# Attention output with queries on partitions and denominators as a V column, turned through DRAM

## The chip, the cores and the metric

The kernel runs on one core of a Trainium2 chip. A core has a matrix engine (PE, TensorE) that multiplies a stationary operand, loaded into the array by a weight load, with a moving operand, and writes to PSUM; a vector engine (DVE), an activation engine (ACT) and GpSimd (POOL) that work element by element; and SP, which here only issues DMAs. Each engine has its own instruction stream and works through it strictly in the order in which it was written; the streams meet at semaphores. A DMA is issued by an engine's queue and carried out by 16 DMA engines that all queues share.

The metric is the device time of one execution, in microseconds (us). Times of one instruction are in nanoseconds (ns) where that is marked.

## The reference, cut to what matters

The reference is one transformer block on a sequence of 2048 tokens with 448 features: a modulated layernorm, a sliding dilated attention with 16 heads of 28 features, a residual, a second modulated layernorm and an MLP (448 to 1792 to 448) with another layernorm in front, and a second residual. The part that the change touches is this:

```python
qkv = (h @ wqkv).reshape(B, S, 3, H, Dh)            # q, k, v: 16 heads of 28
idx = pos[:, None] - (arange(8) * 2)[None, :]       # 8 keys, two apart, back from the query
logits = einsum('bhsd,bhswd->bhsw', q, k[idx]) * Dh ** -0.5   # masked where idx < 0
attn = softmax(logits, axis=-1)
o = einsum('bhsw,bhswd->bhsd', attn, v[idx])
x = x + ga * (o.reshape(B, S, 448) @ wo)
```

Since keys are two apart, even and odd tokens never meet: the kernel treats them as two sequences of 1024 tokens with a dense window of 8 keys. `ga` is a row of 448 numbers, computed from the conditioning vector `c`; the kernel multiplies it into `wo` once.

## The kernel before, in words

**Layout.** The 2048 tokens are 16 blocks of 128 (8 of even, 8 of odd tokens). `front_ln` normalizes a block, turns it on PE (`ptr`) and writes the features-on-partitions array `hT`; `front_qk` makes `qT` and `kT` from it (`pq`, L640). Attention runs in 9 steps, `attention(b)`, b = 0 to 8. A step holds two superblocks (n = 0, 1) of 114 queries, and a superblock two windows (j = 0, 1) of 57 queries that see 64 keys each.

**One attention step.** `values` (L692) makes V for the 128 keys of a superblock's two windows: DVE first copies the two overlapping windows of `hT` side by side into `hw` (L702), then four matmuls with `hw` as the 128-column stationary operand and `Wv` as moving operand (448 columns) accumulate V into `pv` (L708), and ACT copies it to `vbuf`, head by head, each head padded from 28 to 32 columns with zeros (L712). `lmm` (L733) computes the logits, keys on partitions: 64 small matmuls `lt`, each on a 32x64 part of the array. ACT takes the exponential (`et`, L743, two halves) and DVE multiplies with the band mask (L751, two halves). `dmm` then does two things, on 64x32 parts of the array: a matmul with a matrix of ones sums `et` over keys (`pd`, L765, 8 matmuls of 464 columns, 12 in the steps with a sequence's first window) and 64 matmuls with V as stationary operand give the unnormalized output `po` (L773), head features on partitions and queries along the free axis. ACT turns the sums into reciprocals with a logarithm and an exponential (L785, L788); DVE multiplies (L798, two halves) and writes `oT`, which already has features on partitions.

**After attention.** `out_proj(t)` for each of the 16 token blocks takes 128 columns of `oT` as stationary operand and `wo_s` as moving operand, four matmuls `pw` (L814). `wo_s` keeps each head's 28 rows in a group of 32, so it is loaded by four DMAs into a tile zeroed by POOL, and scaled by `ga` on DVE (L676). The result goes through the residual (L818), two layernorms on DVE and POOL, and a DMA transpose from `ybuf` to `yT` (L840). `mlp(j)` works on two token blocks at a time: 56 matmuls with `w1` (`p`, L864), GELU on ACT, 28 matmuls with `w2` (`p`, L885), the last residual (L892) and the store (L905).

**Order.** Nothing runs in the order of the source. Every piece of work is an `add(engine, cost, function, ...)`; a planner (`Planner`) makes a list schedule from the costs written in these calls, from buffer counts (`ROOM`) and from an assumed extra delay of each DMA (`late`), tries it with 60 perturbed rankings, and emits each engine's stream in the order of the best. It adds a cost `SWITCH` when PE changes the way its array is divided (`mode`). So each stream is fixed before the run, and changing one cost can reorder all of them. `PHASES` says which attention steps are followed by which MLP pairs; ACT loads another function table between the two kinds. Dummy matmuls (`pwm`, L506) fill PE's early waits. `mods` computes the modulation rows (`pb`), sends them through a DRAM tile `mod_hbm` to get them onto all partitions (`mod_bc`, L671), and issues the loads of the MLP weights after that (`load_mlp`). All DMAs but one are issued by SP.

**DMA semaphores.** The DMAs of SP take eight semaphores in turn. A DMA that is to use a semaphore waits until the DMA eight places ahead of it has landed.

Of the kernel before, what the change touches and what calls it, by code (L numbers as in the profile page):

```python
# [11 lines left out]
FP32 = mybir.dt.float32  # L12
# [18 lines left out]
OTW = NSB * SBQ  # L31
NBLK = S // 128
EPS = 1e-5
DEN_SCALE = 2.0 ** -32
# [12 lines left out]
LMM, DMM = 0.55, 0.80  # L47
FILL_UNTIL, FILL_SHARE = 12.0, 1.0
ROOM = {"L": 2, "S": 4, "et": 2, "den": 2, "zh": 6, "yT": 3, "hm": 3, "vb": 4, "hw": 3}
# [229 lines left out]
def kernel(  # L279
# [41 lines left out]
    oT = cst.tile([128, 4, OTW], BF16, name="oT")  # L321
    Wv = cst.tile([128, KT, D], BF16, name="Wv")
    Wqk = cst.tile([128, KT, 2, H, HP], BF16, name="Wqk")
    wo_s = cst.tile([128, 4, D], BF16, name="wo_s")
# [12 lines left out]
    ones_k = cst.tile([128, 2, HP], BF16, name="ones_k")  # L337
    neg_half = cst.tile([128, 4], FP32, name="neg_half")
    den_bias = cst.tile([128, 1], FP32, name="den_bias")
# [19 lines left out]
    vbufs = [cst.tile([128, H, HP], BF16, name=f"vbuf{i}") for i in range(NV)]  # L359
# [65 lines left out]
    zero(1.6, lambda: wo_s[:], ["wo"], eng="POOL", rank=440)  # L425
    wo_v = A_wo.rearrange("(ft r d) n -> r d ft n", r=4, d=DH)
    for r in range(4):
        load(lambda r=r: nc.sync.dma_start(out=wo_s[HP * r:HP * r + DH, :, :], in_=wo_v[r]), D * D // 2, [f"wo{r}"],
             reads=["wo"])
# [38 lines left out]
    pool(0.1, lambda: nc.gpsimd.memset(den_bias[:], math.log(DEN_SCALE)), ["den_bias"])  # L468
# [18 lines left out]
    def consts():  # L487
        for vb in vbufs:
            nc.gpsimd.memset(vb[:, :, DH:HP], 0.0)
        nc.gpsimd.memset(ones_k[:], 1.0)  # L490
        nc.gpsimd.memset(ones_k[0:WIN - 1, 1, :], 0.0)

    pool(0.9, consts, ["ones", "vpad"])
# [10 lines left out]
    def dummy(n):  # L504
        for k in range(n):
            nc.tensor.matmul(pwm.t[:, k % 2, :], lhsT=warm_w[:, 0:128], rhs=warm_w[:], start=True, stop=True)  # L506
# [148 lines left out]
    def mods():  # L655
# [19 lines left out]
        for i in range(2):  # L675
            add("DVE", 0.55, lambda i=i: nc.vector.tensor_tensor(  # L676
                out=wo_s[:, 2 * i:2 * i + 2, :], in0=wo_s[:, 2 * i:2 * i + 2, :],
                in1=ga_bc.unsqueeze(1).to_broadcast([128, 2, D]), op=ALU.mult),
                reads=["ga"] + [f"wo{r}" for r in range(4)], writes=[f"wos{i}"], port=True)
# [12 lines left out]
    def values(sb_i):  # L692
# [3 lines left out]
        vbuf = Buf("vb", lambda k: vbufs[k], "vb")  # L696
        pv = ps_one([128, D], "pv")
        hw = sb("hw", [128, KT, 2, WK], BF16, "hw")

        def windows():  # L700
            h = hT[:, :, k0:k0 + WK]
            nc.vector.tensor_copy(out=hw.t[:], in_=bass.AP(h.tensor, h.offset, [h.ap[0], h.ap[1], [WQ, 2], [1, WK]]))  # L702

        P.wrote(add("DVE", 0.21, windows, port=True, reads=PADK + [f"h{kt}_{t}" for kt in range(KT) for t in tb], bufs=[hw]), hw)

        def vmm():
            for kt in range(KT):
                nc.tensor.matmul(pv.t[:], lhsT=hw.t[0:KE[kt], kt].rearrange("p j k -> p (j k)"), rhs=Wv[0:KE[kt], kt, :],  # L708
                                 start=(kt == 0), stop=(kt == KT - 1))

        P.wrote(add("PE", 0.757, vmm, reads=["wva", "wvb", "Wv0"], bufs=[pv, vbuf, hw]), pv)
# [5 lines left out]
    def attention(b, tbl, prev_w1):  # L717
# [4 lines left out]
        et = sb("et", [128, 4, 2, 4, WE], BF16, "et")  # L722
# [19 lines left out]
        for half in range(2):  # L742
            ex = add("ACT", 0.825, lambda half=half: nc.scalar.activation(  # L743
                out=et.t[:, 2 * half:2 * half + 2].rearrange("p r n ft c -> p r (n ft c)"),
# [4 lines left out]
            def msk(half=half):  # L749
                ev = et.t[:, 2 * half:2 * half + 2].rearrange("p r n ft c -> p (r n ft) c")  # L750
                nc.vector.tensor_tensor(out=ev, in0=ev, in1=mask[:], op=ALU.mult)  # L751

            add("DVE", 0.56, msk, port=True, bufs=[et], reads=["mask"], writes=[(et, half)])
        pd = ps_big("pd")
        pos = [ps_one([128, 2, 4, WQ], "po") for _ in range(2)]
        first = [s % (NSB // 2) == 0 for s in sbs]

        def dmm():
            for j in range(2):
                rows = slice(WK * j, WK * j + WK)  # L760
                edge = j == 0 and any(first)
                for n0, n1 in ((0, 1), (1, 2)) if edge else ((0, 2),):
                    ones = ones_k[rows, 1 if edge and first[n0] else 0, :]
                    for r in range(4):
                        nc.tensor.matmul(pd.t[HP * r:HP * r + HP, j, n0 * SBE:n1 * SBE], lhsT=ones,  # L765
                                         rhs=et.t[rows, r, n0:n1].rearrange("p n ft c -> p (n ft c)"),
                                         start=True, stop=True, tile_position=(WK * j, HP * r))
            for n in range(2):
                for ft in range(4):
                    for j in range(2):  # L770
                        rows = slice(WK * j, WK * j + WK)
                        for r in range(4):
                            nc.tensor.matmul(pos[j].t[HP * r:HP * r + HP, n, ft, :],  # L773
                                             lhsT=vb[n].t[rows, ft * 4 + r, :], rhs=et.t[rows, r, n, ft, 0:WQ],
                                             start=True, stop=True, tile_position=(WK * j, HP * r))

        P.wrote(add("PE", DMM, dmm, dense=0.3, reads=[(et, 0), (et, 1), "ones"], bufs=[et, *vb, pd, *pos], mode="64x32"), pd, *pos)
        lt_mms.append(P.tasks[-1])
        lden = sb("den", [128, 2, 2, 4, WE], FP32, "lden")
        rden = lden  # L780

        def flat(t):
            return t[:].rearrange("p j n ft c -> p j (n ft c)")

        P.wrote(add("ACT", 0.825, lambda: nc.scalar.activation(out=flat(lden.t), in_=pd.t[:, :, 0:2 * SBE], func=ACT.Ln,  # L785
                                                               scale=DEN_SCALE),
                    bufs=[pd, lden], order_after=[tbl]), lden)
        ex = add("ACT", 0.92, lambda: nc.scalar.activation(out=rden.t[:], in_=lden.t[:], func=ACT.Exp, scale=-1.0,  # L788
                                                           bias=den_bias[:]),
                 bufs=[lden], reads=["den_bias"], order_after=[tbl])  # L790
        P.wrote(ex, rden)
        exps.append(ex)
        o0 = b * 2 * SBQ

        def div(j):
            out = oT[:, :, o0 + j * WQ:o0 + j * WQ + WQ]
            out = bass.AP(out.tensor, out.offset, [out.ap[0], [SBQ, 2], out.ap[1], [1, WQ]])
            nc.vector.tensor_tensor(out=out, in0=pos[j].t[:],  # L798
                                    in1=rden.t[:, j, :, :, 0:WQ], op=ALU.mult)

        for j in range(2):
            add("DVE", 0.55, lambda j=j: div(j), bufs=[pos[j], rden],
                writes=[f"o{o0 + n * SBQ + j * WQ + i}" for n in range(2) for i in range(WQ)])


    y_of = {}

    def out_proj(t):
        c0 = t // 8 * (OTW // 2) + t % 8 * 128
        pw = ps_one([128, D], "pw")  # L810

        def mm():
# [168 lines left out]
```

## Time and profile before

| | |
|---|---|
| time, median of 2 runs | 186.7 us (186.02 and 187.38) |
| profiled execution, span from first to last instruction | 184.8 us |
| the profiled execution's time outside its span | not recorded; the two timed runs are 1.2 and 2.6 us above the span |
| PE busy with matmuls | 173.5 us, 94% |
| DVE, ACT, POOL busy | 124.6, 103.8, 47.5 us |
| first matmul with `w1` | 54.0 us |
| last matmul ends | 180.6 us |
| granted TensorE clock | full from 7.8 us on |

The profile is of one execution. Busy time is the time in which an engine has at least one instruction under way; a matmul's recorded duration holds its run through the array, so matmuls that follow each other overlap, and the rate is read from start to start or from the pieces of the chain of waits. The chain is followed back from the last instruction: at each step to what released it, or to the instruction ahead of it on its engine. An idle time whose releaser is "issue" is one in which the engine waited for nothing that the profile shows. A DMA's time to landing is counted from its issue to its last completion mark.

### The profile page before, as it was taken

Reading aid. Unit: us, or ns where it says so; the run is one execution under the profiler, and the core shown is the slowest. Engines: PE = TensorE matmul, PEld = TensorE weight load, DVE = VectorE, ACT = ScalarE, POOL = GpSimd, SP = SyncE. Lnnn points to the kernel's source line nnn. Section 1 sums busy time; section 2 is a strip of 40 time slices with the busy share of each in tenths; the row PEclk is TensorE's granted clock in tenths of the full one; section 3 lists DMA queues with packets and bytes.
Section 4 is the critical chain, followed back from the end, with each engine's and each line's share of the span. In section 5 each row is a group of like instructions: output and inputs, shape, how many; then the busy total and the mean of one; then the engine's idle time right before and its main releaser. Section 6 shows DMA issues by size and latency. Waiting matters only on the chain.

```text
span 184.8 us, 5433 instructions
## 1 busy us (share of the span) xinstructions
PE 173.5 (94%) x2325; PEld 111.5 (60%) x2333; DVE 124.6 (67%) x348; ACT 103.8 (56%) x139; POOL 47.5 (26%) x97
## 2 busy tenths in 40 slices
PE   3997789899999999999999999999999999999991
PEld 0574565455458655775855567678556756857750
DVE  3799599889899799688424389693346968711102
ACT  2167667767486877766585667426786530521230
POOL 7074000508501602334200060532001526200000
PEclk9999999999999999999999999999999999999999
DMA  5999779900110101301210100213001012040101
GB/s 172 304 356 265 193 175 313 326 14 7 27 32 0 28 5 32 82 0 28 42 18 0 52 5 4 57 50 48 14 4 53 0 32 78 0 103 7 51 0 50
DMA packets 19004, 13.99 MB, mean 76 GB/s; under 512 B 9246, under 2 KB 18403, under 8 KB 18980
## 3 DMA queue, kind: packets, MB, share of 16 engines
q1 hardware_dynamic: 18978, 13.64, 27.7%
q8 instruction: 18, 0.29, 0.7%
q14 instruction: 6, 0.05, 0.1%
q10 hardware_dynamic: 2, 0.00, 0.0%
HBM read 9.70 MB, written 1.84 MB: 62 GB/s over the span
## 4 chain that ended last, share of the span: by engine, by line
PE 90%; DVE 4%; issue 2%; DMA 1%; ACT 1%; DVEq 0%
PE p L864 27%; PE p L885 23%; PE pq L640 13%; PE pv L708 7%; PE pw L814 7%; PE pwm L506 3%; PE lt L733 3%; PE po L773 3%; PE ptr L607 1%; PE pd L765 1%; DMA yT<-ybuf 1%; DVE st_all L513 1%; DVE kT L649 1%; ACT lden L788 1%; PE pb L661 0%
## 5 line engine op out<-in xcount | busy, mean ns | idle before, releaser
L864 PE MATMUL p<-yT,w_s 128*128 128x256 bf16 x448 | 52.3, 272 | 0.1
L871 ACT ACTIVATE hm<-p 128x1024 bf16<-128x1024 f32 (+1 forms) x32 | 28.8, 916 | 36.8 <-PE p L864 36.8
L864 PEld LDWEIGHTS <-w_s 128*128 128x128 bf16 x448 | 43.3, 97 | 8.9 <-issue 0.6
L885 PE MATMUL p<-w_s,hm 128*128 128x448 bf16 x224 | 46.9, 353 | 0.0
L531 POOL TENSOR_TENSOR rs_all<-tv_all,neg_half 128x1 f32<-128x1 f32 (+1 forms) x35 | 20.9, 605 | 52.3 <-DVE tv_all L528 47.5
L885 PEld LDWEIGHTS <-hm 128*128 128x128 bf16 x224 | 21.2, 98 | 17.9
L844 POOL TENSOR_TENSOR x1p_ring<-x_all,gbb_bc 128x448 f32<-128x448 bf16 x16 | 17.2, 1079 | 54.6 <-DVE x_all L818 45.3
L640 PE MATMUL pq<-hT,Wqk 128*128 128x512 bf16 (+3 forms) x153 | 30.0, 334 | 0.5 <-issue 0.2
L892 DVE TENSOR_TENSOR x_all<-p,x1p_ring 128x448 bf16<-128x448 f32 x16 | 9.8, 618 | 26.0 <-PE p L885 26.0
L640 PEld LDWEIGHTS <-Wqk 128*128 128x128 bf16 (+1 forms) x160 | 15.1, 97 | 11.5 <-DVE Wqk L626 0.2
L513 DVE BATCH_NORM_STATS2 st_all<-x_all 128x6 f32<-128x448 bf16 x32 | 19.1, 617 | 0.7 <-DMA x_all<-in_A_x_dram 0.5
L743 ACT ACTIVATE et<-lt 128x928 bf16<-128x928 f32 x18 | 16.0, 941 | 5.0 <-PE lt L733 4.9
L708 PE MATMUL pv<-Wv,hw 128*128 128x448 bf16 x72 | 16.4, 353 | 1.6 <-DVE hw L702 0.9
L751 DVE TENSOR_TENSOR et<-et,mask 128x928 bf16<-128x928 bf16 x18 | 11.7, 649 | 5.3 <-ACT et L743 5.3
L814 PE MATMUL pw<-wo_s,oT 128*128 128x448 bf16 x64 | 14.4, 352 | 0.0
L712 ACT CAST vbuf<-pv 128x448 bf16<-128x448 f32 x18 | 9.6, 532 | 6.3 <-PE pv L708 6.2
L818 DVE TENSOR_TENSOR x_all<-pw,x_all 128x448 bf16<-128x448 f32 x16 | 9.9, 620 | 4.4 <-PE pw L814 4.2
L785 ACT ACTIVATE lden<-pd 128x928 f32<-128x928 f32 x9 | 8.5, 948 | 7.1 <-PE pd L765 7.1
L652 ACT CAST kT<-pq 128x512 bf16<-128x512 f32 (+1 forms) x14 | 7.1, 510 | 8.6 <-PE pq L640 8.2
L708 PEld LDWEIGHTS <-hw 128*128 128x128 bf16 x72 | 6.7, 97 | 7.7 <-issue 1.2
L798 DVE TENSOR_TENSOR oT<-po,lden 128x456 bf16<-128x456 f32 x18 | 10.6, 623 | 0.6 <-ACT lden L788 0.6
L833 DVE BATCH_NORM_STATS2 st_all<-h 128x6 f32<-128x448 bf16 x16 | 9.8, 621 | 0.1
(83 smaller groups left out, 172.3 us busy)
## 6 DMA issues: line engine op xcount, KB each, us to landing
out_dram<-x_all SPq DMA_DIRECT2D x8, 224.0 KB, 2.0
w_s<-in_B_w_dram SPq DMA_DIRECT2D x2, 784.0 KB, 12.3
wmod<-in_w_mod_dram SPq DMA_DIRECT2D x2, 672.0 KB, 7.5
w_s<-in_B_w_dram SPq DMA_DIRECT2D x1, 1344.0 KB, 9.1
x_all<-in_A_x_dram SPq DMA_DIRECT2D x1, 896.0 KB, 7.9
wm_st<-in_w_mod_dram SPq DMA_DIRECT2D x1, 720.0 KB
wqk_st<-in_A_wqkv_dram SPq DMA_DIRECT2D x2, 339.0 KB, 5.7
x_all<-in_A_x_dram SPq DMA_DIRECT2D x2, 224.0 KB
```

What stands on the lines that cost most here:

```text
L513: add("DVE", 0.53, lambda: nc.vector.bn_stats(out=st_all[:, sl, :], in_=src()), reads=key, writes=[f"st{sl}"])
L531: lambda: nc.gpsimd.tensor_tensor(out=rs_all[:, which, b0:b0 + n], in0=tv_all[:, which, b0:b0 + n], in1=neg_half[:, 0:n], op=ALU.pow),
L640: nc.tensor.matmul(pq.t[:], lhsT=wqk_m(kt, m), rhs=hT[0:KE[kt], kt, c0:c0 + n], start=(kt == 0), stop=(kt == KT - 1))
L708: nc.tensor.matmul(pv.t[:], lhsT=hw.t[0:KE[kt], kt].rearrange("p j k -> p (j k)"), rhs=Wv[0:KE[kt], kt, :], start=(kt == 0), stop=(kt == K ...
L743: ex = add("ACT", 0.825, lambda half=half: nc.scalar.activation(out=et.t[:, 2 * half:2 * half + 2].rearrange("p r n ft c -> p r (n ft c)") ...
L751: nc.vector.tensor_tensor(out=ev, in0=ev, in1=mask[:], op=ALU.mult)
L798: nc.vector.tensor_tensor(out=out, in0=pos[j].t[:], in1=rden.t[:, j, :, :, 0:WQ], op=ALU.mult)
L814: nc.tensor.matmul(pw.t[:], lhsT=oT[:, ft, c0:c0 + 128], rhs=wo_s[:, ft, :], start=(ft == 0), stop=(ft == 3))
L844: nc.gpsimd.tensor_tensor(out=x1p_ring[:, t % NX1P, :], in0=x_all[:, t, :], in1=gbb2_bc[:], op=ALU.add)
L864: nc.tensor.matmul(p1.t[:, f // 2, f % 2 * 256:f % 2 * 256 + 256], lhsT=w1_s[0:kp, kt, (fq + f) * 128:(fq + f + 1) * 128], rhs=yT.t[0:kp, ...
L871: gl = add("ACT", 0.18 + nf * 0.183, lambda fq=fq, nf=nf, p1=p1: nc.scalar.activation(out=hm.t[:, fq:fq + nf, :], in_=p1.t[:, 0:nf // 2, : ...
L885: nc.tensor.matmul(p2.t[:], lhsT=hm.t[:, ft, bi * 128:(bi + 1) * 128], rhs=w2_s[:, ft, :], start=(ft == 0), stop=(ft == FT - 1))
```

## The change

It is four edits that belong together.

1. `values` no longer copies windows. Eight matmuls take the two windows straight from `hT` as stationary operands of 64 columns each, one on the left and one on the right half of the array (parts of 128x64). `hw` and its DVE copy go.
2. `vbuf` gets ones in the columns behind each head's 28 features. `pmm` takes the place of `dmm`: 64 matmuls on 64x64 parts of the array, with `et` as stationary operand (64 keys by 64 queries) and 29 columns of V as moving operand, so that queries come out on partitions, 28 features and the denominator side by side. `pd`, `ones_k`, the logarithm and the exponential on ACT go; DVE takes a reciprocal of 32 columns and one product of 896 columns.
3. The output now has queries on partitions and has to be turned. Four DMAs of 57 rows by 512 columns per step store it to a DRAM tile `o_hbm`; `out_proj` starts with a DMA transpose of 128 rows from there to `oT`. Both are issued by SP.
4. `wo_s` has plain rows (three full groups of 128 and one of 64), loaded by two DMAs and scaled in three instructions. The dummy matmuls work on two halves of the array. Constants, costs and `ROOM` follow.

```diff
-LMM, DMM = 0.55, 0.80
+LMM, PMM = 0.55, 0.60
...
-        P.wrote(add("DVE", 0.21, windows, port=True, reads=PADK + ..., bufs=[hw]), hw)
...
-                nc.tensor.matmul(pv.t[:], lhsT=hw.t[0:KE[kt], kt].rearrange("p j k -> p (j k)"), rhs=Wv[0:KE[kt], kt, :],
-                                 start=(kt == 0), stop=(kt == KT - 1))
+                for j in range(2):
+                    nc.tensor.matmul(pv.t[WK * j:WK * j + WK, :], lhsT=hT[0:KE[kt], kt, k0 + WQ * j:k0 + WQ * j + WK],
+                                     rhs=Wv[0:KE[kt], kt, :], start=(kt == 0), stop=(kt == KT - 1), tile_position=(0, WK * j))
...
+        def pmm():
+            for ft in range(4):
+                for r in range(4):
+                    h = 4 * ft + r
+                    for n in range(2):
+                        for j in range(2):
+                            rows, col = slice(WK * j, WK * j + WK), j if n == 0 else 1 - j
+                            e0 = ((r * 2 + n) * 4 + ft) * WE
+                            nc.tensor.matmul(po.t[WK * col:WK * col + WK, n, HP * h:HP * h + DH + 1],
+                                             lhsT=et.t[rows, e0:e0 + WK], rhs=vb[n].t[rows, h, 0:DH + 1],
+                                             start=True, stop=True, tile_position=(WK * j, WK * col))
...
+        P.wrote(add("DVE", 0.2, lambda: nc.vector.reciprocal(out=rden.t[:], in_=heads()[:, :, :, DH]), bufs=[po, rden]), rden)
+        P.wrote(add("DVE", 1.02, lambda: nc.vector.tensor_tensor(
+            out=osb.t[:, :, 0:D].rearrange("p n (h e) -> p n h e", h=H), in0=heads()[:, :, :, 0:DH],
+            in1=rden.t[:].unsqueeze(3).to_broadcast([128, 2, H, DH]), op=ALU.mult),
+            bufs=[po, rden, osb], reads=["opad"]), osb)
+            def store(n=n, par=par, i=i):
+                for j in range(2):
+                    col, q0 = j if n == 0 else 1 - j, i * SBQ + j * WQ
+                    nc.sync.dma_start(out=o_hbm[par, q0:q0 + WQ, :], in_=osb.t[WK * col:WK * col + WQ, n, :])
+            add("SP", 0.15, store, bufs=[osb], writes=[f"o{par}_{i * SBQ + k}" for k in range(SBQ)], late=2.2)
...
+        P.wrote(add("SP", 1.2, lambda: nc.sync.dma_start_transpose(out=oT.t[:], in_=o_hbm[par, r0:r0 + 128, :]),
+                    reads=[f"o{par}_{r0 + i}" for i in range(128)], bufs=[oT], late=1.8), oT)
```

## The prediction

> **What bounds the kernel now.** I read the stretches first: each engine's busy time from 10 us to the first matmul with `w1` at 54.0, and from there to the end.
>
> ```profile
> core 0: us, PE busy (x) PEld busy (x) DVE busy (x) ACT busy (x) POOL busy (x), PEclk, DMA share, GB/s
> 10.00:54.00 44.00, 39.67 (x645) 23.38 (x647) 39.44 (x111) 30.17 (x53) 14.28 (x46) 1.00 0.62 173
> 54.00:180.00 126.00, 125.79 (x1620) 84.49 (x1625) 78.04 (x209) 70.88 (x82) 28.80 (x40) 1.00 0.13 29
> ```
>
> After 54 PE is never idle (125.79 of 126.00): there only PE's own work counts. Between 10 and 54 PE idles 4.33 us, and DVE is as full as PE. So an edit that spares DVE and ACT can win at most those 4.3 us; anything more must come off PE. Next the chain of waits, for what a piece of PE work costs:
>
> ```profile
> 63.50 0.76 PE p L885 x4
> 64.25 0.63 PE lt L733 x64
> ...
> 68.28 0.86 PE p L885 x4
> ...
> 70.76 0.32 PE pd L765 x8
> 71.08 0.55 PE po L773 x64
> 71.63 0.49 PE p L885 x2
> ```
>
> Four `w2` matmuls take 0.76, but 0.86 behind `lt`; two take 0.49 behind `po`, where 0.38 would be the rate. Each change of the array's division costs 0.1 us (start to start in the trace, 95 ns). `po` is 64 pairs of weight load and matmul at 8.3 ns.
>
> Last the DMA issues, with us to landing:
>
> ```profile
> out_dram<-x_all SPq DMA_DIRECT2D x8, 224.0 KB, 2.0
> w_s<-in_B_w_dram SPq DMA_DIRECT2D x2, 784.0 KB, 12.3
> ...
> mod_bc<-mod_hbm SPq DMA_DIRECT2D x1, 448.0 KB, 4.7
> ...
> yT<-ybuf SPq DMA_TRANSPOSE x16, 2.4
> ...
> w_s<-in_B_b_dram SPq DMA_DIRECT2D x1, 3.5 KB
> ```
>
> An undisturbed store lands in 2.0, a transpose in 2.4. But the MLP weights, issued from 23.57 to 28.9, land until 38.3, and the 3.5 KB row `b1`, issued at 24.60 among them, has its completion mark only at 32.2, when the `w1` load ahead of it is nearly through. A small transfer behind the loads waits for them.
>
> **PE's work.** (1) V: eight matmuls of 448 columns, two side by side, should take as long as four. The nearest row is `pb` (L661): 16 matmuls of 448 columns on four 128x32 parts take 0.87, 0.19 a round, so parts with the same rows run side by side. I take 0.76 as before. If they did not, V would double. (2) In the order of the two built programs, PE changes its division 39 times before and 61 times after, since V now has one of its own: 15 to 29 times ahead of the first `w1` matmul, 24 to 32 behind. 22 x 0.095 = +2.1. (3) `pd` and `po` take 0.87 with the change behind them. `pmm` has 64 pairs again: 0.54 at the rate of `po`, 0.63 at that of `lt`; with four parts at work instead of eight, at worst twice `lt`, 1.26. I take 0.6, near the rows, plus 0.1 for the change behind it: -0.17 a step, -1.5 in all (bounds -2.1 and +4.4). The other work is the same. So PE's work does not shrink: +0.6, and behind 54, where only that counts, 0.76 (one V moved there from ahead of the first `w1`) + 0.76 (8 changes) - 1.0 (6 steps) = +0.5.
>
> **DVE and ACT.** ACT loses 0.95 + 1.07 per step, 18 us; DVE loses 18 `hw` copies of about 0.2 from start to start (3.7) and trades two products of 0.53 for one of 896 columns (two L798, 1.06; between 1.0 and 1.3) and a reciprocal (145 ns for 4 columns, L554; 0.1 to 0.5 for 32, I take 0.15). Behind 54 this is worth nothing, PE covers it. Ahead it could lift the 0.9 us in which V waits for `hw` at 15.2.
>
> **What I cost at nothing.** The dummies stream as many columns, in pairs on two halves of the array, and fill waits for the first loads. `wo_s` comes in two DMAs instead of four and needs no zeroing; its three scalings (128x896, 128x448, 64x448) replace two of 0.61 with the same columns. POOL's constants grow by about 1 us (six more clears like L489's 0.15): hidden, since POOL idles between its powers, but for the power of blocks 4 to 7, which could come at 19.5, when DVE gets to it; without that cover up to 1 us of DVE goes, into the step below.
>
> **The new path, step by step.** I follow the order of the changed program with durations from these rows. Step 0 is somewhat earlier than before: `po` ends near 19.3 (21.3 before), the product near 21.0. SP then issues two stores, `mod_hbm`, two stores, at 0.45 each (the `out` rows take 0.37 to 0.53 to issue), to 23.4. `mod_bc` needs `mod_hbm` landed (2.0 behind its issue): 24.4, against 23.16. Next in SP's stream stands the transpose of token block 0, which waits for the last two stores: 25.5, and takes SP 1.2. The MLP loads stand behind it: 26.75 instead of 23.57. From the issue of `mod_bc` to the last weight 15.1 us passed before, with the DMA engines busy throughout; the same again, with a transpose between, ends at 40.0.
>
> Two waits follow. **First**, on DVE: the scaling of `wo_s`, which needs `mod_bc` (24.4 + 4.7 = 29.1), stands ahead of the second mask product of step 1, and DVE waits with it. The mask is done near 30.5 and `po` of step 1 can start at 30.6; PE is through with the work ahead of it at 28.2. That is 2.4 us of PE idle. **Second**, on SP: the product of step 1 ends near 33.3; its first store is issued at 33.4, behind `w2`, and lands when the loads do, 40 to 41. The transpose of token block 1 waits for that store, and lands 2.4 later, near 43. PE, with 8 us of `pq`, V and `pw` after `po`, comes to `pw` of block 1 at 39.3: 3.6 us of idle. Other waits on this way (for the transposes of x, for masks) I put at 2.3 together, and half of the 2.0 us of "issue" idle that `po` shows before at 1.0: 9.3 idle against 4.3. Ahead of the first `w1` matmul: +5.0 idle, +1.3 (14 changes), -0.5 (3 steps), -0.76 (one V fewer) = **+5.0**; it starts near 59. Block 1's way from `pw` to `yT`, 12.3 to its transpose before, just fits.
>
> **The later turns.** From the end of `po` to the landed transpose: 0.2 to wake DVE, 1.3 for reciprocal and product, 0.4 to 1.6 of issues, 2.0, 2.4 and 0.3 of wakes: 6.6 to 7.8. The changed order gives PE 8.2 us of other work between `po` of step 3 and the first `pw` that needs it, 8.7 to 10.6 in steps 4 to 8. The cover holds by 0.4 to 2 where DVE is free at once. I charge 0.5 for all of them (0 to 4). Cover gone, each microsecond a store takes longer costs a microsecond per step.
>
> Sum: 5.0 + 0.5 + 0.5 = +6.0: a span of 190.8. The timed runs have a median 1.9 above the profiled span; I carry that over: 186.7 + 6.0 = **192.7**.
>
> **A rule on the stores.** The Trainium skill (DMA: Bandwidth & Descriptors, section "Why a DMA increments its semaphore by 16 and not by 1") says that a transfer runs on the largest number of engines up to 16 that divides its outer dimension: 3 for 57 rows. The trace agrees where it can: the 28-row loads of `wo` leave 14 completion marks, the 4-row `mod_hbm` 4; no run shows 57. By an estimate from that page and the 41 ns of an 896-byte packet here, the four stores of a step put 76 rows on the same three engines, 3.1 us, and the last lands some 1.5 later than I assume; the sum would be near 196 (third rival).
>
> **Rivals.** *Not slower:* the first store of step 1 passes the loads. It is decided at `pw` of block 1: if its transpose lands before PE comes there at 39.3, the 3.6 us are gone: 189.1; if the loads also start early enough that `wo_s` does not hold the mask, 2.4 more: 186.7. I say **188.3** (187 to 190.4). For it: the store goes to DRAM, not from it, and uses few engines. Against it: `b1`. Chance 0.29.
> *Faster:* PE's early idle vanishes (-4.3) and pairs run at `po`'s rate (-2.1): near **182**. Against it: two new DMA trips in just that stretch. 0.05.
> *Late turns at every step:* if a store takes 4.7, like `mod_bc`, instead of 2.0, the trip is 9.3 to 10.5, up to 2 us over the cover; with half of that for six steps +4 to +6: **197**. 0.07.
> *The clock drops:* it is full from 7.8 on, and PE's longest idle after 10 is 1.3; it falls 4.7 us after the last matmul. A wait of 3.6 is between. At the start it took 5.0 us of dummies (0.45 each, then 0.25) to come up: 2.5 us lost, **195.2**. The Trainium skill (TensorE: Matmul & The Clock Gate, section "HAM oscillation — how this bites in real kernels") puts the drop at idle gaps above about 3.4 us; by that rule this wait would bring it. 0.06.
> *The change does not do what it says:* V's halves run one after the other, 18 x 0.76 = +13.7, **206**. `pb` speaks against it. 0.02.
>
> **Numbers.** The forecast has 0.51, with a range of its own of 190.5 to 195. About 2%, 183.0 to 190.4, is what a measurement of this kernel can tell from no change. Slower by more: 0.51 + 0.07 + 0.06 + 0.02 = 0.66; within: 0.29; faster: 0.05. The range from 187.2 to 196.5 holds the forecast, nearly all of the first rival and most of the clock's.
>
> **What would show it.** In the changed profile: `w1` first near 59; PE idle at `pw` near 40, released by a DMA of `oT`, and at `po` near 28, released by DVE; the weight loads issued near 26.8; PE full afterwards; `pmm` 0.6, V 0.76 with 0.1 at its edges. Wrong if the store lands within 3 us of its issue, if PE stalls at `pw` all along, or if V takes 1.5.

## The result, and the profile after

| | before | after |
|---|---|---|
| time, median of 2 runs | 186.7 us (186.02 and 187.38) | 206.4 us (206.32 and 206.47) |
| profiled execution, span | 184.8 us | 204.8 us (its time: 206.47) |
| first matmul with `w1` | 54.0 us | 65.2 us |
| from there to the recorded end of the last matmul (180.9 and 201.0) | 126.9 us | 135.8 us |
| PE idle from 10 us to the first `w1` / behind it | 4.3 / 0.2 us | 11.8 / 5.9 us |
| TensorE clock at half from 10 us on, in this execution | never | 10.2 us, ahead of the first `w1` |

The changed kernel is slower by a factor of 1.104 (95% interval 1.092 to 1.116); a second measurement beside other runs gave 1.098 (1.089 to 1.108). The forecast was 192.7 us, with a range to 196.5: the direction was right, the size was not. I read the views in the order in which I read those of before. First the page's span, busy times and granted clock:

```profile
span 204.8 us, 5584 instructions
...
PE 180.4 (88%) x2373; PEld 111.5 (54%) x2380; DVE 122.4 (60%) x331; ACT 85.9 (42%) x121; POOL 47.2 (23%) x101
...
PEclk9999997975999999999999999999999999999999
```

ACT has lost 18 us as worked out, and PE has gained 7 of busy time. The clock row has three slices of 5 us below full speed; in the profiled execution of before there was none:

```profile
PEclk9999999999999999999999999999999999999999
```

Next the stretches up to the first `w1` matmul and from there:

```profile
10.00:65.16 55.16, 43.33 (x648) 22.97 (x648) 42.76 (x117) 27.13 (x49) 15.13 (x52) 0.91 0.59 161
65.16:200.60 135.44, 129.58 (x1615) 83.17 (x1619) 72.76 (x188) 56.48 (x68) 28.90 (x40) 1.00 0.23 49
```

In the first stretch PE is busy 43.3 of 55.2 us, and its mean clock is 0.91. In the second, where before PE was busy all the time, 5.9 us are missing, and its work has grown from 126.3 to 129.6. Third, the waits of PE (line, what it waited for, us in total, times, longest):

```profile
PE pw L797 <- DMA oT<-o_hbm: 6.8, 4, 4.4
PE p L847 <- DMA yT<-ybuf: 5.8, 3, 2.8
...
PE po L761 <- DVE et L748: 1.6, 2, 1.3
```

Both large ones are transposes: that of the new turn, and that of the old `yT`. No DMA stands among PE's waits of before, whose largest from 10 us on were:

```profile
PE po L773 <- issue: 2.0, 2, 1.3
PE pv L708 <- DVE hw L702: 0.9, 1, 0.9
```

The chain of waits (start, length, what) tells how they come about:

```profile
24.43 3.79 DMA mod_bc<-mod_hbm
28.25 0.69 DVE wo_s L677 x2
28.94 0.55 DVE et L748
...
32.42 8.92 DMA o_hbm<-os
41.36 2.92 DMA oT<-o_hbm
44.33 1.78 PE pw L797 x4
...
59.43 5.68 DMA yT<-ybuf
65.16 6.33 PE p L847 x56
71.48 1.83 PE pw L797 x8
```

`mod_bc` holds the scaling of `wo_s` and that the mask (`et`); the first store of step 1 takes 8.92 us to land among the MLP weights; its transpose releases `pw` of block 1 at 44.33. So far it is the path of the prediction. What was not in it: SP needs from 32.42 to 37.92 just to issue the four stores of step 1, 5.5 us, against 1.4 in step 2; four `pw` matmuls take 1.78 there, at half clock; the `yT` ahead of the first `w1` matmul takes 5.68 instead of 2.4, since the four stores of step 2 were issued just in front of it (57.96 to 58.98) and land 2.4, 3.2, 5.0 and 5.4 behind their issue; and eight `pw` matmuls take 1.83 where before they took 1.51:

```profile
106.28 1.51 PE pw L814 x8
```

### The profile page after: what moved, and what is told of

It reads as the page before. It is cut to its first block, busy times and chain, and to the rows that moved or that the text cites. A ratio compares the mean times of both kernels' runs of the same rounds, so it can differ in the third digit from the quotient of the medians.

```text
span 204.8 us, 5584 instructions
## 1 busy us (share of the span) xinstructions
PE 180.4 (88%) x2373; PEld 111.5 (54%) x2380; DVE 122.4 (60%) x331; ACT 85.9 (42%) x121; POOL 47.2 (23%) x101
## 4 chain that ended last, share of the span: by engine, by line
PE 63%; DMA 20%; DVE 12%; ACT 2%; issue 1%; DVEq 0%; SPq 0%
PE p L847 22%; PE p L868 18%; PE pq L641 6%; DMA o_hbm<-os 6%; DMA yT<-ybuf 6%; PE pw L797 5%; DMA oT<-o_hbm 5%; PE pv L704 4%; PE lt L730 3%; DVE os L771 2%; DMA mod_bc<-mod_hbm 2%; DVE et L748 1%; PE po L761 1%; DMA mod_hbm<-mod_rows 1%; DVE st_all L514 1%
## 5 line engine op out<-in xcount | busy, mean ns | idle before, releaser
L847 PE MATMUL p<-yT,w_s 128*128 128x256 bf16 x448 | 51.5, 272 | 6.0 <-DMA yT<-ybuf 5.8
L854 ACT ACTIVATE hm<-p 128x1024 bf16<-128x1024 f32 (+1 forms) x32 | 28.6, 916 | 63.1 <-PE p L847 58.1
L868 PE MATMUL p<-w_s,hm 128*128 128x448 bf16 x224 | 45.8, 353 | 0.0
L532 POOL TENSOR_TENSOR rs_all<-tv_all,neg_half 128x1 f32<-128x1 f32 (+1 forms) x35 | 22.3, 644 | 62.7 <-DVE tv_all L529 57.4
L641 PE MATMUL pq<-hT,Wqk 128*128 128x512 bf16 (+3 forms) x153 | 31.1, 349 | 1.1 <-issue 0.7
L797 PE MATMUL pw<-wo_s,oT 128*128 128x448 bf16 x64 | 17.7, 381 | 6.8 <-DMA oT<-o_hbm 6.8
L704 PE MATMUL pv<-Wv,hT 128*64 128x448 bf16 (+1 forms) x144 | 16.9, 363 | 0.0
L797 PEld LDWEIGHTS <-oT 128*128 128x128 bf16 x64 | 5.6, 99 | 18.0 <-DMA oT<-o_hbm 8.3
L653 ACT CAST kT<-pq 128x512 bf16<-128x512 f32 (+1 forms) x14 | 7.0, 510 | 13.7 <-PE pq L641 13.5
L653 ACT CAST qT<-pq 128x512 bf16<-128x512 f32 (+1 forms) x15 | 7.5, 501 | 11.0 <-PE pq L641 10.8
L704 PEld LDWEIGHTS <-hT 128*64 128x64 bf16 (+1 forms) x144 | 6.9, 111 | 7.3 <-issue 4.0
L771 DVE TENSOR_TENSOR os<-po,rden 128x896 bf16<-128x896 f32 x9 | 9.7, 1082 | 0.1
```

What stands on the lines that cost most here:

```text
L532: lambda: nc.gpsimd.tensor_tensor(out=rs_all[:, which, b0:b0 + n], in0=tv_all[:, which, b0:b0 + n], in1=neg_half[:, 0:n], op=ALU.pow),
L641: nc.tensor.matmul(pq.t[:], lhsT=wqk_m(kt, m), rhs=hT[0:KE[kt], kt, c0:c0 + n], start=(kt == 0), stop=(kt == KT - 1))
L653: add("ACT", 0.13 + n / 1400, lambda dst=dst, pq=pq: nc.scalar.copy(out=dst, in_=pq.t[:]), bufs=[pq], writes=w)
L704: nc.tensor.matmul(pv.t[WK * j:WK * j + WK, :], lhsT=hT[0:KE[kt], kt, k0 + WQ * j:k0 + WQ * j + WK], rhs=Wv[0:KE[kt], kt, :], start=(kt == ...
L771: P.wrote(add("DVE", 1.02, lambda: nc.vector.tensor_tensor(out=osb.t[:, :, 0:D].rearrange("p n (h e) -> p n h e", h=H), in0=heads()[:, :, ...
L797: nc.tensor.matmul(pw.t[:], lhsT=oT.t[0:KW[kt], kt, :], rhs=wo_s[0:KW[kt], kt, :], start=(kt == 0), stop=(kt == KT - 1))
```

## The experiments

Kernels that were run together share runs of the kernel before on the same chip (medians 186.5 to 187.9), so ratios are compared, not microseconds. The columns of PE are in us and come from one profiled execution per kernel (for `k65`, `no_wait` and `act_stores` the longest of its four, 206.03, 204.81 and 213.29 us); half clock counts from 10 us to the last matmul. Unless said otherwise, the order of the instructions on the compute engines is that of the changed kernel.

| kernel | time | ratio (95%) | first `w1` | PE idle ahead / behind | half clock |
|---|---|---|---|---|---|
| after, again | 206.21 | 1.098 (1.089 to 1.108) | 62.9 | 9.8 / 5.6 | 6.8 |
| no_turn | 193.24 | 1.027 (1.018 to 1.037) | 55.2 | 3.6 / 2.5 | 3.4 |
| no_turn_k65 | 190.17 | 1.017 (1.011 to 1.022) | 52.7 | 3.6 / 2.5 | 0 |
| no_wait | 202.29 | 1.077 (1.067 to 1.087) | 63.6 | 10.9 / 4.2 | 10.2 |
| loads_after | 200.78 | 1.065 (1.056 to 1.074) | 58.1 | 6.9 / 4.2 | 6.8 |
| spread | 204.14 | 1.086 (1.078 to 1.093) | 61.3 | 8.9 / 4.7 | 10.2 |
| k65 | 204.17 | 1.082 (1.072 to 1.091) | 64.1 | 11.0 / 6.7 | 10.2 |
| k65_loads | 197.55 | 1.055 (1.046 to 1.064) | 56.5 | 6.7 / 5.9 | 3.4 |
| fixed | 198.76 | 1.065 (1.059 to 1.072) | 59.0 | 8.0 / 4.9 | 3.4 |
| act_stores | 211.67 | 1.131 (1.121 to 1.141) | 64.9 | 11.4 / 8.7 | 20.5 |
| clock | 209.18 | 1.121 (1.113 to 1.129) | 63.5 | 7.6 / 6.5 | 17.1 |
| v_alone | 187.66 | 1.0056 (1.0030 to 1.0081) | 54.6 | 2.4 / 0.3 | 0 |
| replanned | 210.89 | 1.11 to 1.14 (single runs) | 62.5 | 4.8 / 12.5 | 13.7 |
| best | 199.95 | 1.071 (1.067 to 1.075) | 55.9 | 6.1 / 8.7 | 13.7 |
| act_best | 214.64 | 1.149 (1.141 to 1.158) | 64.9 | 13.5 / 13.5 | 17.1 |

### How much hangs on the turn: no_turn and no_wait

My theory was that the turn through DRAM costs the time, and by waits: a transpose that waits until stores have landed. The rival was the work on PE. `no_turn` leaves the turn out.

```diff
-                    nc.sync.dma_start(out=o_hbm[par, q0:q0 + WQ, :], in_=osb.t[WK * col:WK * col + WQ, n, :])
+                    pass
...
-        P.wrote(add("SP", 1.2, lambda: nc.sync.dma_start_transpose(out=oT.t[:], in_=o_hbm[par, r0:r0 + 128, :]),
+        P.wrote(add("SP", 1.2, lambda: None,
...
-                nc.tensor.matmul(pw.t[:], lhsT=oT.t[0:KW[kt], kt, :], ...
+                nc.tensor.matmul(pw.t[:], lhsT=oT_0[0:KW[kt], kt, :], ...     # a constant tile
```

> The changed kernel with the same order on every engine, but the four stores of a step and the 16 transposes from DRAM are left out; the output projection reads a constant tile, so the attention output does not enter the result. Theory (waits for the turn, and the clock that falls in them, make most of the loss): PE's waits for oT (6.8) and the yT waits behind the stores (5.8) go, and with them most of what the half clock cost (about 4): 190 to 193 us, first w1 matmul at 53 to 56. Rival (the added changes of the array's division and the new matmul forms on PE make it): 200 or more, PE still busy over 180 us.

1.027 instead of 1.10: of the 19.7 us some 13 to 14 hang on the turn. That leaves open whether it is the dependency or the traffic. `no_wait` keeps every store and every transpose, but the transposes read a block of zeros that was written once at the start.

```diff
-        ... nc.sync.dma_start_transpose(out=oT.t[:], in_=o_hbm[par, r0:r0 + 128, :]),
+        ... nc.sync.dma_start_transpose(out=oT.t[:], in_=z_hbm[:]),
```

> The changed kernel with all its stores and transposes, but the transposes read a block of zeros in DRAM, written once at the start, instead of what the stores wrote: the attention result is left out of the output, and no transpose waits for a store any more. Theory 1 (dependency): pw of block 1 and the yT ahead of the first w1 matmul find their data in time or nearly; close to the kernel without stores and transposes, 1.03 to 1.045. Theory 2 (traffic): transposes still land late behind weights and 57-row stores in the DMA engines, pw of block 1 still waits 3 us or more, and the time stays at 1.07 to 1.10.

1.077 against 1.098 of the changed kernel on the same chip: without the wait for the stores' landing only 2.1 points (hundredths of the ratio; 4 us) of the 7.1 that separate the changed kernel from `no_turn` go. Theory 2 holds. The waits and the chain of `no_wait`:

```profile
PE pw L799 <- DMA oT<-z_hbm: 7.0, 2, 5.3
PE p L849 <- DMA yT<-ybuf: 4.0, 2, 2.2
...
37.87 6.33 DMA oT<-z_hbm
44.20 0.05 issue
44.24 1.78 PE pw L799 x4
```

The transpose of block 1 waits for no landing now, is issued at 37.87, and still lands 6.33 later, behind the weights and four stores: `pw` starts at 44.24, in the changed kernel at 44.33. What I had taken for a chain of two landings is a transfer that comes late there even if it waits for no store. The two are not quite separated: in SP's stream the transpose still stands behind the four stores of its step, and is issued as soon as SP is through with them. Behind the first `w1` the transposes of the turn take 2.9 to 6.4 us, where stores are under way.

### The queue behind the weights: loads_after and act_stores

`loads_after` issues the four large loads of `w1` and `w2` behind the transpose of block 2.

```diff
+        def turn():
+            nc.sync.dma_start_transpose(out=oT.t[:], in_=o_hbm[par, r0:r0 + 128, :])
+            if t == 2:
+                late_loads()          # the four loads of w1 and w2, no longer issued behind mod_bc
```

> The changed kernel, same order on the compute engines, with the four big loads of w1 and w2 issued behind the transpose of token block 2 instead of ahead of the stores of step 1. Theory (the first store of step 1 lands 8.9 us behind its issue because it stands behind these loads): it lands in about 2.5, PE's wait of 4.4 for oT of block 1 goes, and with it the second stretch of half clock (2.9 lost): 199 to 201, first w1 matmul near 58 to 60. Rival (what holds the first w1 matmul is the way through DVE to yT, not the store): 204 to 206.

1.065: 6 to 7 us of the turn's price come from putting it into the stretch in which the weights land. The stores of step 1 now land 2.2 to 4.6 us behind their issue instead of 6.5 to 8.9, and `pw` of block 1 no longer waits. `act_stores` leaves the loads where they are and issues the stores on another engine's queue.

```diff
-                    nc.sync.dma_start(out=o_hbm[par, q0:q0 + WQ, :], ...
+                    nc.scalar.dma_start(out=o_hbm[par, q0:q0 + WQ, :], ...
```

> The changed kernel with the stores of the turn issued by ACT on its own queue instead of by SP; nothing else, the same order on PE and DVE, ACT issues the stores where SP did in the planned order. Theory 1 (the stores of step 1 waited because they stand behind the MLP weights in SP's queue): they now land 2.4 to 5.4 behind their issue, the wait at pw of block 1 falls from 4.4 to under 1, the loads are issued 1.5 earlier, and the first w1 matmul comes near 60: 1.104 to about 1.07. Theory 2 (the DMA engines work off what they have been given, whatever the queue): landing stays at 6.5 to 9 behind the issue, the time at 1.10. Against both: ACT may be held by a store that waits, and exp or gelu with it; then PE waits for hm or et.

```profile
33.24 6.92 DMA o_hbm<-os
40.23 5.48 DMA oT<-o_hbm
59.10 5.80 DMA yT<-ybuf
```

Theory 2 of this run: the four stores of step 1, on a queue that holds nothing else, land 6.5 to 8.1 behind their issue. The order within SP's queue was not what held them. It is slower than the changed kernel: PE waits 1.6 at `pq` for a `vbuf` that ACT delivers late, 3.6 at a `yT` that lands among the stores, and the clock is at half for 20.5 us. The Trainium skill (DMA: Bandwidth & Descriptors, section "Queues, rings and completion order") says that each DMA engine takes turns between the queues packet by packet; by that I would expect small stores on a second queue to pass the weights, and this trace does not show it.

### The 64-row matmul: k65 and no_turn_k65

`wo_s` with plain rows has 448 = 3 x 128 + 64: the last of `pw`'s four matmuls has 64 rows. The edit gives it 65, row 65 being zero.

```diff
-                nc.tensor.matmul(pw.t[:], lhsT=oT.t[0:KW[kt], kt, :], rhs=wo_s[0:KW[kt], kt, :],
+                nc.tensor.matmul(pw.t[:], lhsT=oT.t[0:KE[kt], kt, :], rhs=wo_s[0:KE[kt], kt, :],
```

> The changed kernel, same order, with 65 instead of 64 rows in the last matmul of each output projection (the added row of wo is zero, the result is the same). Theory: the 64-row matmul is run as a change of the array's division, twice 0.095 us around each of the 16: 3.0 us less PE work, 203.4 (202.5 to 204.5), and four matmuls of the projection take 0.76 instead of 0.92. Rival (the extra 0.16 per projection is the wait for a DMA's semaphore ahead of its first weight load): 206.4, still 0.92.

> The kernel without stores and transposes (pw reads a constant tile; the attention result never reaches the output), and besides with 65 rows instead of 64 in the last of pw's four matmuls (row 65 of both operands is zero). Theory: a 64-row matmul is run as a change of the array's division, 0.095 us at either edge, 16 blocks x 2 = 3.0 us, all of it on the path, since PE is not waiting: from 1.027 times the kernel before (without stores and transposes alone) to 1.011, 190.2 us if the kernel before stands at 187.9. What is then left over is V's division changes and the product. Rival: the longer start-to-start behind the 64-row matmul is not a cost of its own (the next matmul would have come no earlier): 1.027, no change.

With the turn in place the gain is 1.7 to 2.2 points, with intervals that touch. Without the turn it is 1.027 to 1.017, and these intervals overlap too; the traces are clear: PE's work behind the first `w1` falls from 129.7 to 127.3 us. The same piece of the chain in `no_turn` and in `no_turn_k65`:

```profile
61.56 1.83 PE pw L795 x8
```

```profile
59.02 1.52 PE pw L796 x8
```

Start to start, 25 of the `pw` matmuls of the changed kernel take 0.28 to 0.29, 3 with 65 rows; the others 0.19. A matmul of 64 rows, written without any division of the array, costs 0.1 at either edge, as a change of division does: at most 32 x 0.1 = 3.2 us in all. In `no_turn` 30 starts of `pw` and what follows it are 0.28 to 0.29 apart, in `no_turn_k65` 3: an estimate of 27 x 0.1 = 2.7 for the whole kernel, beside the 2.4 measured behind the first `w1`.

What `no_turn_k65` still has over the kernel before is not PE's work. Its two stretches are

```profile
10.00:52.69 42.69, 39.13 (x658) 22.83 (x655) 40.01 (x108) 26.79 (x48) 15.06 (x51) 1.00 0.63 179
52.69:182.40 129.71, 127.22 (x1621) 84.12 (x1619) 75.74 (x196) 56.45 (x68) 29.41 (x40) 1.00 0.11 28
```

PE is busy for 166.4 us there, 166.0 in the kernel before (39.7 and 126.3). In this trace the last matmul ends 1.5 us later: PE idles 0.8 less ahead of the first `w1` and 2.3 more behind it, nearly all of it in one wait of 2.26 for a `yT` near the end, to which the section on other orders comes back.

### V alone

> The kernel before with V alone changed: 64-column parts straight from hT, no copied windows; products, denominators and output as before, the order planned anew. Theory: the halves run side by side, and the cost is the division changes, 56 against 37, 19 x 0.095 = +1.8, less up to 0.9 us in which V waited for the window copies ahead of the first w1 matmul: 1.005 to 1.010, 189 us. Rival 1: the halves run one after the other, 18 x 0.76 = +13.7: 1.073. Rival 2: DVE's 18 spared copies are worth more than the changes: 0.99 or below.

```diff
-            nc.vector.tensor_copy(out=hw.t[:], in_=...)                     # the two windows
...
-                nc.tensor.matmul(pv.t[:], lhsT=hw.t[0:KE[kt], kt].rearrange("p j k -> p (j k)"), ...
+                for j in range(2):
+                    nc.tensor.matmul(pv.t[WK * j:WK * j + WK, :], lhsT=hT[0:KE[kt], kt, k0 + WQ * j:k0 + WQ * j + WK], ...
```

This is the first edit of the change alone, in the kernel before. 1.0056: 1.05 us, the division changes less what the spared copies gave (PE idles 2.4 ahead of the first `w1` instead of 4.3). The halves do run side by side: in the changed kernel's chain three V in a row take

```profile
73.95 2.40 PE pv L704 x24
```

three times 0.76 and one edge of 0.12.

### Smaller stores: spread, fixed, k65_loads

All 36 stores of the changed kernel leave three marks of landed data each, so they ran on three DMA engines, and those of one step land one behind the other, 0.8 to 2.2 apart in step 2. `spread` stores 56 rows on their own and the 57th rows extra: 36 large and 27 small DMAs.

```diff
-                    nc.sync.dma_start(out=o_hbm[par, q0:q0 + WQ, :], in_=osb.t[WK * col:WK * col + WQ, n, :])
+                    nc.sync.dma_start(out=o_hbm[par, q0:q0 + WQ - 1, :], in_=osb.t[WK * col:WK * col + WQ - 1, n, :])
+                # and the row q0 + WQ - 1: both of a pair in one DMA where n == 0, else one by one
```

> The changed kernel, same order, with each 57-row store split into 56 rows and the last row (seven stores a step instead of four). Theory (57 rows run on three DMA engines, so four stores of a step run one after the other there, 0.9 us each, and hold the transposes behind them): with 14 engines all stores land in 2.0 to 3.0 instead of 2.4 to 5.4, PE's waits for yT and oT behind the first w1 fall from 8.4 to under 4: 200 to 203. Rival (a store's landing is set by DRAM and the queue, not by the number of engines): the landings stay above 4 and the time stays at 206, or rises by the three added issues a step.

A 56-row store leaves 14 marks; those of step 2 land in 1.5 to 1.6 us, and the `yT` behind them in 2.4 instead of 5.7. In step 1, among the weights, they still take 4.8 to 8.3. 1.086: 1.2 to 1.8 points, with intervals that touch. Then the three repairs together, and two of them without the split:

> The changed kernel with the three repairs together: 65 rows in pw's last matmul, 56 rows of each store on their own and the 57th rows in extra small stores, MLP weights loaded behind the transpose of block 2. Same order on the compute engines. Theory: the three take different things away (PE work; store time; the queue behind the loads): 1.104 - 0.022 - 0.018 - 0.039 = 1.025, or up to 1.04 where the last two shorten the same waits (pw of block 1, the yT ahead of the first w1): 192.5 to 195.5 us with the kernel before at 187.9. Rival: the waits come from the number of DMAs that SP issues in a row (seven stores a step, 0.4 each), which no repair shortens: 1.05 or more.

> The changed kernel with two repairs: 65 rows in pw's last matmul, and the MLP weights loaded behind the transpose of block 2; the stores stay whole (57 rows, three engines). Theory 1 (the split stores bring nothing once the loads are out of the way, since SP issues seven instead of four per step): as fixed or better, 1.045 to 1.065. Theory 2 (the split stores helped there too): 1.07 or more.

`fixed` has the edits of `k65`, `spread` and `loads_after`, `k65_loads` the first and the last. They do not add up: 1.065, which `loads_after` alone has, and without the split stores 1.055. Once the loads are out of the way no gain of the split is left to see (the last two intervals overlap). Two places show where its gain goes. SP issues seven stores a step, and `mod_bc`, behind those of step 0, is issued at 25.8 instead of 24.4. And PE waits elsewhere (`fixed`):

```profile
PE p L866 <- DMA yT<-ybuf: 4.0, 2, 2.2
...
PE po L768 <- DVE et L755: 3.0, 2, 2.0
...
PE pw L816 <- DMA oT<-o_hbm: 2.4, 4, 0.9
```

### Another order: replanned, best, act_best

The planner had been told 0.15 us of SP and 2.2 to land for a pair of stores. `replanned` tells it 0.75 and 4.6; nothing else changes.

```diff
-            add("SP", 0.15, store, bufs=[osb], writes=[...], late=2.2)
+            add("SP", 0.75, store, bufs=[osb], writes=[...], late=4.6)
```

> The changed kernel with one thing other: the planner is told what a pair of stores took in the runs (0.75 us of SP and 4.6 to land, instead of 0.15 and 2.2), and plans the order anew. Theory 1 (the waits behind the first w1 matmul, 5.6 us, are the planner's wrong figures): most of them go, 3 to 5 us: 1.08 to 1.09. Theory 2 (there is not enough other work to put between): the idle time moves elsewhere, 1.10 or more. The wait behind the loads at pw of block 1 stays with both.

`best` adds to the three repairs V as in the kernel before and figures that fit the split stores:

```diff
-            add("SP", 0.15, store, bufs=[osb], writes=[...], late=2.2)
+            add("SP", (1.25, 1.65)[n], store, bufs=[osb], writes=[...], late=1.7)
...
-                    reads=[...], bufs=[oT], late=1.8), oT)
+                    reads=[...], bufs=[oT], late=1.6), oT)
```

> The three repairs, V made as in the kernel before from copied windows (the two first windows of a half keep their own buffers), and the planner told what stores and transposes took in the runs so far (stores 1.25 and 1.65 us of SP per task and 1.7 to land, transposes 1.6), so that the order is planned anew. Theory: PE's work is then the kernel before's less 0.17 a step (1.5 us), 38 division changes against 37, and with the turn covered it comes to 0.99 to 1.01, 186 to 190 us; what it is above 0.99 is turn waits left. Rival: ahead of the first w1 matmul there is not enough other work to cover a turn, whatever the order: 1.02 or more, with PE idle at pw of blocks 0 to 3.

`act_best` has 65 rows, V as before, and the stores as work of ACT:

```diff
-            add("SP", 0.15, store, bufs=[osb], writes=[...], late=2.2)
+            add("ACT", 0.7, store, bufs=[osb], writes=[...], late=4.0)      # issued by nc.scalar
```

> The changed kernel with 65 rows in pw's last matmul, V as in the kernel before, and the stores on ACT's queue, told to the planner as ACT work (0.7 a pair, 4.0 to land), order planned anew. Theory: without turn waits this would come to 1.00 (no stores and transposes, 65 rows: 1.017; V's changes 0.006; the wait for the last yT 0.012); what it shows above that is the turn: 1.01 to 1.03 if ACT's queue is free of the loads. Rival: ACT, which now issues 36 stores of 0.35 and waits for the product each time, becomes late with exp and gelu: 1.05 or more.

None is better than the repairs in the order of the changed kernel, and `best` and `act_best` are far from what their theories expected. The waits of PE in `replanned` and in `best`:

```profile
PE p L847 <- DMA yT<-ybuf: 9.5, 1, 9.5
PE pw L797 <- DMA oT<-o_hbm: 4.8, 2, 2.7
```

```profile
PE p L871 <- DMA yT<-ybuf: 7.8, 1, 7.8
...
PE pw L821 <- DMA oT<-o_hbm: 0.6, 2, 0.3
```

In `best` the waits at `pw` are nearly gone, and one near the end has come in their place, at the `w1` of blocks 12 and 13. From `pw` of block 13 to that `w1` it took 12.0 us in the kernel before (143.95 to 155.93, with PE full), 15.9 in the changed one (161.6 to 177.5, PE idle for 2.2 of them) and 14.0 in `best` (154.3 to 168.3, 7.8 idle). The way is longer because DVE works in order. In the changed kernel `ybuf` of these blocks is begun at 173.20, behind the residuals of blocks 14 and 15 and two of the MLP, the last of which waited for PE's `w2` until 172.66; in the kernel before it was begun at 149.79, ahead of the last two `pw`. The 2.2 us are in `no_turn` too, where the turn is gone and its order is kept: they belong to the order that the planner made for the turn. With `act_best` come waits for ACT and for `hT` (2.6 and 7.2).

### The clock

`clock` puts 18 matmuls (3.4 us) in front of `pw` of block 1, where PE waited 4.4.

```diff
         def mm():
+            for k in range(18 if t == 1 else 0):
+                nc.tensor.matmul(pw.t[:], lhsT=warm_w[:, 0:128], rhs=warm_w[:, 0:D], start=True, stop=True)
```

> The changed kernel with 18 additional matmuls of 448 columns (3.4 us at full clock, their result overwritten) ahead of pw of token block 1, into its own tile: PE works where it waited 4.4 us for the transpose. Theory: the clock stays up, the 6.8 us at half clock from 43.5 on (3.4 us of work lost) go, and the path to the first w1 matmul is shorter by that: 203 us on the clock of the first run, 1.104 to about 1.085. Rival: the yT in front of the first w1 matmul waits behind the stores of step 2 anyway and takes the gain back: 1.10, with that wait longer than 2.8.

```profile
41.48 3.57 PE L797 MATMUL pw<-warm_w 128*128 128x448 bf16 x18
44.89 1.03 PE L799 MATMUL pw<-wo_s,oT 128*128 128x448 bf16 x4
```

At that place it does what it should: no wait, and `pw` takes 1.03 instead of 1.78. The time is not better but worse (1.121 against 1.098). In this run the clock was at half from 29.5 to 36.3, from 63.6 (behind the wait for `yT`), 162.6 and 179.7, each time for 3.41 us or twice that. So the price of the one stretch could not be told from this run.

What the traces show is that each such stretch from 10 us on begins inside a wait of PE or at most 1.9 us behind one, and that not every wait brings one: the 2.2 us wait near the end brought it in `loads_after`, `spread`, `no_wait`, `k65`, `k65_loads`, `act_stores` and `clock`, and not in the two runs of the changed kernel, `no_turn`, `no_turn_k65` and `fixed`. Nor does it take the new waits: in 11 of the 34 executions of the kernel before beside these experiments the mean granted clock was 0.979 to 0.990, about what one or two stretches of 3.4 us at half would make of 186 us (0.991 and 0.982). Their traces are not kept.

## Why the prediction was wrong

The span came out at 204.8 where I had 190.8. The 14.0 by the steps of the prediction:

**PE's work: "the other work is the same".** Wrong, by 2.7 behind the first `w1` (PE's work 126.7 to 129.9 us up to the last matmul, with +0.5 in the sum), of which 2.5 at `pw` (start to start 9.9 to 12.5): the 64-row matmul. I had the rows of `wo_s` in front of me and counted division changes by the operations that ask for one.

**"Block 1's way from `pw` to `yT` just fits."** Wrong, 2.8: the stores of step 2 stand in the DMA engines in front of that `yT`. I had counted stores as something to wait for, not as something in the way of the next transposes.

**"I charge 0.5 for all" later turns.** Wrong by 5.2. PE's idle time behind the first `w1` is 5.9: 3.0 at `yT` (2.2 of it at the end, from the order) and 2.4 at `pw`, the rest at `hm` and in pieces of 0.05. My trip of 6.6 to 7.8 took 2.0 for a landing and 2.4 for a transpose; the last store of a step takes 4.2 to 5.4 and the transposes of the turn 2.5 to 4.7 from step 2 on. The range that I gave, 0 to 4, was too short at its upper end. The third rival had this mechanism and 4 to 6, at 0.07; with the 2.2 of the order taken off, some 3.4 came of it. The Trainium skill's rule behind it (DMA: Bandwidth & Descriptors, section "Why a DMA increments its semaphore by 16 and not by 1"), three engines for 57 rows, agrees with the trace: three marks with each of the 36 stores, 14 with 56 rows.

**"The clock drops", a rival at 0.06.** It dropped, for 10.2 us; 1.4 of them PE was idle, so 4.4 of work were lost. About 1.5 of these fell into the first stretch, ahead of the wait at `pw` of block 1, where slower work makes that wait shorter; so not all 4.4 need have cost time. I had let it hang on the 3.6 us wait alone, but it fell first at 29.8, behind waits of 0.88 and 1.30 with 8 small matmuls between. The Trainium skill (TensorE: Matmul & The Clock Gate, section "HAM oscillation — how this bites in real kernels") speaks of gaps above about 3.4 us. The stretches, each 3.41 or a multiple, fit its window; the threshold, as a single gap, does not: here shorter waits in a row were enough.

**Idle ahead of the first `w1`: 9.3.** 11.8 with the `yT` just told; without it 9.0. `mod_bc` was issued at 24.43 (I had 24.4), the first store of step 1 at 32.42 (33.4), and its transpose landed at 44.28 (43); PE came to `pw` at 39.91 (39.3) and waited 4.4 (3.6). At `po` it waited 0.9 and 1.3 instead of 2.4. These steps were right, but for their reading: `no_wait` shows that the transpose would have been as late without waiting for the store's landing. The landing of 2.0 was too short here already: the last store of step 0 took 3.8, so the weight loads went out at 27.99 (26.75) and had landed at 41.58 (40.0).

**Right:** V side by side; 0.61 for `pmm`; PE's work apart from `pw` (+0.4 in `no_turn_k65`, where I had +0.6); the product at 1.08 (a reciprocal took 0.36, I had 0.15; it lies beside other work).

Added up over the forecast: 2.8 for `yT`, 4.4 for the clock and -1.1 for the rest ahead, 5.2 and 2.7 behind: 14.0. This sorts PE's idle and busy time; it is not what each cause would give back alone, as the repairs show. The third rival and that of the clock were right as mechanisms; I priced them as alternatives to the forecast, where they came together with it.

What stays open: why stores on a queue of their own do not pass the weights (another placement of the weights was tried, smaller weight loads were not), and whether an order exists that hides turn and last `yT` at once. No version tried beats the kernel before. Without any turn and with 65 rows the new products stand at 1.017, and in that trace PE's work is within 0.4 us of the kernel before's: the products cost PE nothing to speak of, but they did not make it faster either.

## What to carry to other kernels

When a step adds DMAs, ask not only who waits for them but which transfers already there come to lie behind them: here dropping the wait for the stores gave back 4 us, moving the weights out of the way 6 to 7. Count a matmul with 64 rows as a change of the array's division, and compare it with one padded to 65. And look where the clock falls: a wait of 2 us can cost more than itself, since half speed for 3.4 us or more may follow it, in one run and not in the next.

## What was not expected of the hardware

- A 64-row matmul without any division asked for takes 0.1 us more at either edge (start to start 0.28 to 0.29 against 0.19); with 65 rows that is gone.
- Small stores on ACT's queue, with 3.1 MB of weights under way on SP's, landed 6.5 to 8.1 us behind their issue, as on SP's own (6.5 to 8.9).
- Four 57-row stores of a step land up to 5.4 us behind their issue with no weights under way, and a transpose behind them in up to 5.7 instead of 2.4; 56-row stores of the same step land in 1.5 to 1.6.
- The clock was at half for 3.41 us or a multiple of it each time, and fell behind waits as short as 0.88 and 1.30 with 8 small matmuls between (0.87 and 0.66 in `no_turn`).
